# New piece costs in a kernel's planner, and a TensorE order searched with them

## The chip, the cores and the metric

The kernel runs on one core of one Trainium2 chip. A core has TensorE (matrix multiplies, here called PE), VectorE (DVE), ScalarE (ACT), GpSimd (POOL), a queue of transfers issued from SyncE (SP), and 16 DMA engines between HBM and the core's own memory. TensorE writes to eight banks of PSUM, from which VectorE and ScalarE copy. The metric is the device time of one execution in microseconds (us); lower is better.

## The reference: what is computed

Two layers of the same kind, each an attention with a recurrent memory followed by a gated feed-forward part, on 2048 tokens of width 576. All inputs are bfloat16. The same weights serve both layers.

```python
def _A_ref(x, mem0, Wq, Wk, Wv, Wo, seg_len):      # seg_len 32, M = 8, 32 heads of 128
    ...
    mem = mem0
    for s in range(n_seg):
        xs = x[:, s * seg_len:(s + 1) * seg_len, :].copy()
        h = jnp.concatenate([mem, xs], axis=1)
        q = jnp.einsum('btd,dhe->bhte', h, Wq)
        k = jnp.einsum('btd,dhe->bhte', h, Wk)
        v = jnp.einsum('btd,dhe->bhte', h, Wv)
        scores = jnp.einsum('bhqe,bhke->bhqk', q, k) * scale
        scores = jnp.where(mask[None, None], scores, -1000000000.0)
        p = _softmax(scores, axis=-1)
        o = jnp.einsum('bhqk,bhke->bhqe', p, v)
        o = jnp.einsum('bhte,hed->btd', o, Wo)
        mem = o[:, :M, :].copy()
        outs.append(o[:, M:, :])
    return jnp.concatenate(outs, axis=1)
...
x = x + _A_ref(_layernorm(x, axis=-1), A_mem0, A_Wq, A_Wk, A_Wv, A_Wo, A_seg_len)
x = x + _B_ref(_layernorm(x, axis=-1), B_w1, B_w3, B_w2)      # (silu(x w1) * (x w3)) w2, 576 -> 4608 -> 576
x = x + _A_ref(_layernorm(x, axis=-1), A_mem0, A_Wq, A_Wk, A_Wv, A_Wo, A_seg_len)
x = x + _B_ref(_layernorm(x, axis=-1), B_w1, B_w3, B_w2)
```

A segment needs the memory that the segment before it leaves, so the 64 segments of a layer come one after the other.

## The kernel before

**Steps.** The second layer runs 8 segments behind the first (`LAG`), so there are 72 steps, and in most of them one step works on a segment of each layer at once: 80 columns (two times 32 tokens and 8 memory columns) go through the same weights. At both ends, steps have one layer only and 40 columns. Heads are worked in four groups of eight. After every four steps the feed-forward part takes a group of 128 tokens of each layer; its weights don't fit beside the attention's and are loaded anew each time in pairs of 128-row blocks (`W13`, `W2C`).

**Pieces.** `make_nodes` (from line 236) lists all work as nodes: each has an engine (or "either ScalarE or VectorE"), an estimated duration, the nodes that it depends on, and the buffers that it takes and frees. On TensorE a node is a piece of 4 to 64 matmuls, and each kind has a letter: Q and q are QK's main part and tail (the width of 576 is four blocks of 128 rows and a tail of 64), S the scores, T a transpose of the softmax on TensorE, P the product with V, O and o the output projection and its tail, V, v, X, x, G, g the V projections, F and f the feed-forward's upper part, W and w its lower part for the first and second layer's tokens, and a, b, n, p the transposes around the layer norms. In steps with both layers the softmax is transposed by DMA instead of T (node `TRD`, from PB to PTS); its planned duration is `TRD` on the queue and `TRL` until it has landed.

**Modes.** A matmul can use the whole 128x128 array ("full"), or two halves of its columns ("col") or of its rows ("row"); the V pieces of the ends also use narrower forms ("c32", "oct", "quad"). Some kinds need one mode: Q and O full, q, f and g row, o and the scores of two layers col. Flexible ones are "full/col": F, W, w, G, P, T and the layer norms' transposes. In col mode the emitter splits each of their matmuls in two, one for each half of the columns.

**The planner.** `plan` (from line 80) goes through the nodes as a list scheduler: it keeps a clock for each engine, takes the node that can start first, and issues every engine's work in the order in which the nodes are planned. So its estimated times set the order on ScalarE, VectorE, GpSimd and SP, and which of ScalarE and VectorE does a copy. TensorE's own order is not chosen there: it is the string `ORDER`, FIRST, then FOUR eleven times, then LAST, one letter for each piece. `plan` adds `SWITCH` (98 ns) when the next piece has no mode in common with the run before it, narrows the run's mode to what all of its pieces share, and sets the mode when the run ends (`settle`). `MORE` holds additions by engine and kind, `LATS` the time from an engine's end to the start of a reader elsewhere. None of these numbers reaches the chip: they act through the order of the instructions, the choice between ScalarE and VectorE, the buffers' numbers and the mode of a piece.

The emitter's `mm` (line 622) records each matmul and splits it in col mode. All matmuls have line 627 in the profile, all ScalarE work line 630 and all VectorE work line 633; tiles tell them apart (HT,W is QK; QKT scores; PTS,V the product with V; OT,WO the output projection; XTB,W and W2C,HTT the feed-forward; WV,HT V).

Of the kernel before, what the change touches and what calls it, by code (L numbers as in the profile page):

```python
# [55 lines left out]
class Node:  # L56
    __slots__ = ("eng", "dur", "fn", "deps", "prio", "mode", "acq", "rel", "name", "lat", "outs", "left", "ready",
                 "start", "end", "by")

    def __init__(self, eng, dur, fn, deps=(), prio=0.0, mode=None, acq=(), rel=(), name="", lat=None):  # L60
# [19 lines left out]
def plan(nodes, pools, letters):  # L80
# [15 lines left out]
    both = []  # L96
    mode, run = [], []
    order = []
# [24 lines left out]
    while len(order) < len(nodes):  # L123
# [76 lines left out]
def ewh(*ns):  # L200
# [4 lines left out]
FIRST = (  # L205
    "maqqQqQSqTQQQSqQqqSQTQqSXxVvPPTTOOPoPOooOoQqqqqQQSQVvSqqQQQTQSqqXTSPOPTPOOTooPoxOoQQqqqqQSQvVqSQqQQQSqqTPSTOPoOT"
    "PTOPooOoaQqqQQSQqqVvSqQQQqqqTSQPxTSOPXOToToPPOOooQqqqpQQSVvqqQQnQSFfqqQTQSPfqFSOTFPfWoTOPFTOPoofOoFfqqQQWSFQQqqf"
    "vVqQSTFqfQWQQSqfqFPFTSXfPWTOPOxoTFoPOOffooFVqqvQQWQSQqqfFQqqfFSQTWSPQqfqFQFSTOfPWoTOPFTOPfaOoooFfqqQQvqqSQQWSfVF"
    "qQqQWQTQPqSqTOPbSOxxXTXTPooPOOooQpQQqqqqQSnQSFfqFfQvqVSfFWQqqQfPSFPOOooFfPWOFPofOoFQqqfqQWQSqqqQQQSFSGfgqQQqgfFP"
    "GSWPGfggfFFGOPoOOPWOoooFFffqqQQWSqqQQFvSqfVqQQfFSWqQQqfPPSFFOOPWoOffFPoaoOoWQqqqqQQbSQQQqqSGSgqQQqgPGSOPGggGoPOO"  # L210
    "PooOoQqqqppQQQqvVSSnnQFfqqQQQfqqSFFSPfPwOOWoFPoffFOwPWOooFqqffQQwFWQQqqFSSFffqqQQQQqqwWSSgfGFPGgggGPGOoPOOPWOooo"
    "wFqfqqQQQQSffqqFFSQQwvqVWSFQqqffFQWPwSFffPOPOOowooWFPFOoafQQqqqWSQqqqQQQSwSbQqQgqGSggGPGPOGoPgOPOOooo"
)
# [4 lines left out]
LAST = (  # L218
    "QqqppQQSQqqqvVSQQnqqnQSFPqffQOoSPFOFPwWOFPfooOofQQQqqqfFSwWQQFfqqfFSwWqqQQSGqffgFQFPGgWSwPFggfGOOPoGowPOOooFvfqq"
    "VQQQQSWqqFSFqqffQQQQqqSPwWSFfPOOoWwFffPFPOOooowQWQfqqqFSFfqqQQQWSqqqQQSQbvVVSPwXvxPOPOoOPooOoQQppVqqqQQSqvqnQSnQ"  # L220
    "qffFFQTSqqQTPwFfSPWTOOPFffTFooOPWwOooFffqvVQWFQQqqqQSwSQQfqqFSTFfqqQQWTPwSPFOTOffoPTFoPOOWoowxvXVqqQQFSQqfqqQQSF"
    "QQqqqfQTwPSTSWOPFOffTFPToWoPOwOooFqqfvQQQSQqqfVwWSFFfQqqQTWqSPQQqTOSPbOxooTXPTwPOOooQQpqqqQSqQVvnSqqQQqQSQFfqTFP"
    "STfOPoTOwPTFPOOooofVvqqQQQqqSQQSFfqqFQQSTwqqQTFPffSPOTOwxXooPTFPOOffooFQQqqqqQSQFSfvVqqQQQTqqSQwTPfSOFPFTOwTooPf"
    "POfOooFvVQQqwQqqqSQqqQSQfFTSqQqQfPTSPOOooFTTPPfOOoopwfFFnFwffFFwffFFwwffFfFwFfFwffFfFwFfFwffFFwffFFwffFw"
)
# [10 lines left out]
def make_nodes(em, nseg, pools, o=Opt, dma_bw=230e3, load_bw=400e3):  # L236
# [125 lines left out]
    def step(t):  # L362
# [18 lines left out]
        for g in range(NG):  # L381
            qs, qe = [], []
            for u in (2 * g, 2 * g + 1):
                q = Slot("qkt", users=1)
                b = banks()
                pq = t + o.qk + o.ustep * u
                m_ = node("PE", 32 * mm80, em.qk(t, u, b), deps=hx + hm[:1] + ([ld_h[u // 4]] if t == 0 else []),
                          prio=pq, mode="full", acq=[q] + b, name="QK")
                n = node("PE", 4 * mm80, em.qk_tail(t, u, b), deps=hx + hm + ([ld_h[u // 4]] if t == 0 else []), prio=pq + o.qkt, mode="row",
                         acq=[q] + b, name="QKt")  # L390
# [22 lines left out]
            if nl == 2 and g < DMA_GROUPS:  # L413
                pe_ = [node("DMA", TRD, em.ptd(t, g, pb, pts), deps=[pbs], prio=pf, acq=[pts], rel=[pb], name="TRD", lat=TRL)]
                pts_of[t, g] = pe_[0]
            else:
                bt = banks(nl)
                tr = node("PE", 8 * (0.0258 if nl == 1 else 0.0358), em.ptr(t, g, pb, bt), deps=[pbs], prio=pf + o.tr, mode="full/col", acq=[pts] + bt, rel=[pb], name="TR", lat=0.265)
# [14 lines left out]
            wo = node("PE", 32 * mm80, em.wo(t, g, ot), deps=ote + ([ld_o[g]] if t == 0 else []), prio=t + o.wo + o.wog * g, mode="full",  # L433
                      acq=[y] if g == 0 else [], name="WO")
# [35 lines left out]
    def job(j):  # L470
# [36 lines left out]
        for at, pp in enumerate([npp - 1] + list(range(npp - 1)) if last else range(split, npp)):  # L507
# [5 lines left out]
            for pr_ in (2 * pp, 2 * pp + 1):  # L513
# [18 lines left out]
                fm = node("PE", 16 * mm, em.ffn_up(ents, pr_, w13, b, last and not stays, False), deps=wr + ld, prio=prio, mode="full/col",  # L532
                          acq=b + [htt], rel=rel13, name="FF")
                ff = node("PE", 2 * mm, em.ffn_up(ents, pr_, w13, b, last and not stays, True), deps=wr + ld, prio=prio + o.fft, mode="row",
# [6 lines left out]
            for (bi, g) in ents:  # L541
                b = banks()
                d = node("PE", 8 * 0.1225, em.ffn_down(em.col(bi, g), pp, htts, w2s, b, last and not stays), deps=mids + lds, prio=prio + o.w2,
                         mode="full/col", acq=b, rel=htts + w2s, name="W2b" if bi else "W2")
                if last and at == npp - 1:
# [847 lines left out]
```

## Time and profile before

| | |
|---|---|
| median of 3 runs | 2644.31 us |
| lowest, highest run | 2639.14, 2650.45 us |
| profiled execution, its own time | 2638.71 us |
| its span (first to last instruction) | 2636.9 us |
| mean granted TensorE clock | 0.996 |
| read from HBM, over the span | 306.72 MB, 117 GB/s |

The profile is of one execution. Busy time of an engine is the time in which at least one of its instructions ran; matmuls overlap in the array, and their ends are modelled, so the start of one piece to the start of the next tells more of its cost than its listed length. The chain of waits follows the last instruction back to what released it, step by step. A wait is listed with the engine and line that waited, what it waited for, and the total, the number and the longest. Numbers such as 128*64 in a matmul's shape are the rows and columns of the array that it used, so 128*64 is col mode, 64*128 row mode and 128*128 full.

### The profile page before, as it was taken

The numbers are of one execution on the slowest core, as the hardware profiler recorded it, in microseconds if no ns is written. First come the engines' busy times: TensorE is split into PE (matmuls) and PEld (weight loads), VectorE is DVE, ScalarE is ACT, GpSimd is POOL, SyncE is SP. The second block draws the span as 40 slices with busy tenths as digits, with TensorE's granted clock in tenths as the row PEclk, the third lists the DMA queues.
The fourth block names the chain that finished last, engine by engine and source line by source line (L and its number), as shares of the span: only waits on it lengthen the run. The fifth ranks groups of instructions, "written<-read, shape, count | busy, mean of one in ns | idle before, by whom it ended". The sixth has DMA issues, their size and how long they took to land.

```text
span 2636.9 us, 134690 instructions
## 1 busy us (share of the span) xinstructions
PE 2574.1 (98%) x60031; PEld 2222.3 (84%) x60031; DVE 2004.5 (76%) x5137; ACT 1264.2 (48%) x3745; POOL 196.7 (7%) x253
## 2 busy tenths in 40 slices
PE   5999999999999999999999999999999999999998
PEld 4788888889888888888888888888888888888886
DVE  4787777887778678777877777787777777777876
ACT  2655553444445454444545444454545445454552
POOL 1100000000000010000001001000100001010000
PEclk9999999999999999999999999999999999999999
DMA  9065755575464656546454654655465464545357
GB/s 324 4 174 135 190 104 147 130 148 139 126 147 115 139 127 155 136 131 151 113 140 116 159 140 128 155 110 139 114 156 143 132 159 94 139 122 146 106 156 247
DMA packets 683207, 371.56 MB, mean 141 GB/s; under 512 B 233753, under 2 KB 672801, under 8 KB 681985
## 3 DMA queue, kind: packets, MB, share of 16 engines
q1 hardware_dynamic: 678944, 355.00, 53.2%
q8 instruction: 469, 7.68, 1.2%
q0 software_dynamic: 3024, 6.93, 0.9%
q10 hardware_dynamic: 656, 1.02, 0.2%
q14 instruction: 114, 0.93, 0.1%
HBM read 306.72 MB, written 2.36 MB: 117 GB/s over the span
## 4 chain that ended last, share of the span: by engine, by line
PE 91%; DVE 4%; DMA 3%; issue 1%; ACT 1%; ACTq 0%; DVEq 0%; SPq 0%
PE bank L627 91%; DMA PTS<-PB 2%; DVE HTT L633 1%; DVE PB L633 1%; DVE STAT L633 1%; DMA WV<-in_A_Wv_dram 0%; DVE SME L633 0%; DMA W<-in_A_Wk_dram 0%; DVE V L633 0%; DVE QKT L633 0%; DMA W2C<-in_B_w_dram 0%; DVE XR L633 0%; ACT HTT L630 0%; ACT HT L630 0%; DVE LNS L633 0%
## 5 line engine op out<-in xcount | busy, mean ns | idle before, releaser
L627 PEld LDWEIGHTS <-W 128*128 128x128 bf16 (+2 forms) x32920 | 1261.8, 101 | 119.8 <-issue 67.8
L627 PE MATMUL bank<-HT,W 128*128 128x80 bf16 (+3 forms) x23040 | 795.2, 197 | 21.3 <-ACT HT L630 8.2
L627 PE MATMUL bank<-XTB,W 128*64 128x256 bf16 (+5 forms) x9880 | 658.4, 264 | 2.1 <-issue 1.3
L630 ACT ACTIVATE QKT<-bank 128x256 bf16<-128x256 f32 (+4 forms) x1676 | 385.1, 309 | 302.9 <-PE bank L627 296.5
L627 PE MATMUL bank<-OT,WO 128*128 128x80 bf16 (+3 forms) x11520 | 411.6, 198 | 2.5 <-issue 1.9
L627 PEld LDWEIGHTS <-WO 128*128 128x128 bf16 (+1 forms) x11520 | 383.2, 102 | 29.9 <-issue 16.3
L630 ACT ACTIVATE V<-bank 64x512 bf16<-64x512 f32 (+1 forms) x603 | 338.0, 584 | 137.4 <-PE bank L627 131.4
L627 PE MATMUL bank<-WV,HT 128*32 128x512 bf16 (+4 forms) x3576 | 363.5, 384 | 0.3 <-issue 0.2
L627 PE MATMUL bank<-W2C,HTT 128*64 128x288 bf16 (+1 forms) x3440 | 323.8, 287 | 0.5 <-DMA W2C<-in_B_w_dram 0.5
L630 ACT ACTIVATE HTT<-bank 128x512 bf16<-128x512 f32 (+1 forms) x322 | 172.6, 551 | 300.1 <-PE bank L627 299.1
L633 DVE TENSOR_REDUCE STAT<-SME 104x8 f32<-104x320 f32 (+1 forms) x576 | 274.9, 477 | 28.2 <-ACT SME L630 21.2
L633 DVE TENSOR_TENSOR PB<-SME,STAT 40x128 bf16<-40x128 f32 (+4 forms) x912 | 274.8, 335 | 9.3 <-DMA PTS<-PB 0.5
L627 PEld LDWEIGHTS <-HT 128*32 128x32 bf16 (+4 forms) x3576 | 149.2, 99 | 147.7 <-issue 37.8
L633 DVE SCALAR_TENSOR_TENSOR HTT<-HTT,bank 128x512 bf16<-128x512 bf16 (+1 forms) x322 | 201.0, 624 | 94.4 <-ACT HTT L630 91.6
L627 PEld LDWEIGHTS <-HTT 128*64 128x64 bf16 (+1 forms) x3512 | 233.1, 106 | 31.2 <-DVE HTT L633 4.1
L1047 POOL MEMSET PB<- 128x1024 bf16 x142 | 135.0, 952 | 1657.0 <-DMA PTS<-PB 1114.3
L633 DVE SCALAR_TENSOR_TENSOR XR<-bank,XR 128x288 f32<-128x288 f32 x574 | 240.0, 447 | 20.3 <-PE bank L627 17.2
L630 ACT ACTIVATE OT<-bank 128x320 bf16<-128x320 f32 (+1 forms) x383 | 144.4, 404 | 214.5 <-PE bank L627 185.3
L630 ACT ACTIVATE SME<-SME 104x320 f32<-104x320 f32 (+1 forms) x288 | 135.5, 470 | 194.3 <-DVE SME L633 192.4
L633 DVE TENSOR_TENSOR HTT<-HTT,bank 128x512 bf16<-128x512 bf16 (+1 forms) x322 | 203.3, 631 | 28.5 <-PE bank L627 1.4
L633 DVE CAST V<-bank 64x512 bf16<-64x512 f32 (+1 forms) x261 | 178.9, 686 | 40.1 <-PE bank L627 34.9
L633 DVE TENSOR_TENSOR SME<-bank,maskb 104x320 f32<-104x320 f32 (+1 forms) x288 | 138.5, 482 | 53.8 <-PE bank L627 50.1
(59 smaller groups left out, 1383.5 us busy)
## 6 DMA issues: line engine op xcount, KB each, us to landing
W<-in_B_w_dram SPq DMA_DIRECT2D x608, 256.0 KB, 3.6
W2C<-in_B_w_dram SPq DMA_DIRECT2D x304, 288.0 KB, 3.4
W<-in_B_w_dram SPq DMA_DIRECT2D x608, 32.0 KB, 3.4
W<-in_B_w_dram SPq DMA_DIRECT2D x8, 1024.0 KB, 12.6
W<-in_A_Wq_dram SPq DMA_DIRECT2D x9, 512.0 KB, 9.9
WO<-in_A_Wo_dram SPq DMA_DIRECT2D x4, 1152.0 KB, 19.1
XR<-in_A_x_dram POOLq DMA_DIRECT2D x16, 288.0 KB, 3.1
WV<-in_B_w_dram SPq DMA_DIRECT2D x4, 1152.0 KB, 7.5
```

The source lines that it names most:

```text
L627: self.ch("PE", self.nc.tensor.matmul(out, lhsT=lhsT, rhs=rhs, start=start, stop=stop, skip_group_check=True, **k))
L630: self.ch("ACT", self.nc.scalar.activation(*a, **k))
L633: self.ch("DVE", getattr(self.nc.vector, fn_)(*a, **k))
L1047: return lambda n: self.ch("POOL", self.nc.gpsimd.memset(self.pbt(pb), 0.0))
```

## The change

It touches numbers of the planner, one rule in it, and the order string. No computation, buffer or transfer is added or removed.

- Node gets a field `wide`: an extra cost of a flexible piece if its run ends up col. `plan` adds these up over a run and charges them once the run can only be col.
- `wide` is set for VG (0.01 us), TR (0.04), PV (0.014 with two layers, 0.045 with one), FF (0.02) and W2 (0.01).
- Costs of single pieces change: scores of two layers, WO tails and VG count less; scores of one layer, QK and WO of one layer and QK tails count 8 to 22 ns more.
- Transfers are planned shorter: the transposed softmax's landing 2.1 us after its 1.3 on the queue instead of 2.3, W13 and W2 loads 0.2 us shorter.
- FIRST, FOUR and LAST have the same letters as before, each in another order.

```diff
-        "PE": {"SC": 0.05, "WOt": 0.03, "VG": 0.03, "FFt": 0.01, "TR": 0.01, "QK": 0.007}}
+        "PE": {"SC": 0.0, "WOt": 0.022, "VG": 0.003, "FFt": 0.01, "TR": 0.01, "QK": 0.007}}
...
-TRD, TRL = 1.3, 2.3
+TRD, TRL = 1.3, 2.1
...
-        self.lat = lat
+        self.lat, self.wide = lat, wide
...
-    mode, run = [], []
+    mode, run, owed = [], [], 0.0
...
                 dur += SWITCH
                 settle()
-                mode = n.mode
+                mode, owed = n.mode, 0.0
             mode = [m for m in mode if m in n.mode]
+            owed += n.wide
+            if mode == ["col"]:
+                dur += owed
+                owed = 0.0
             run.append(n)
...
 FOUR = (
-    "QqqqppQvVSQQnnQFqfqFSfqqQQFfqQSWPwPSFffOOowFPWoOPFOooFqfqfQQwQQqqgSWGSFqqfQQQPwQSWFqffqFSGgggGPGPOOwooOPWOooFFqq"
-    "ffQQQQSwVvqqfFSQQqqWPFSFfqqfQQwOSWPFFoffPOOWPwOoooFfqqQQqqaSQQqWSQQqqqQQSbwSggGGPGPOggoGPOPOOooo"
+    "QqqqppQVvSQQnnQqqFSffqFQQQqqfSFPWwSPOFoffOFPwWOPFOoooFqffqQQQQqqSWwGSFfqqgQQQPWQSwFffqqFGSgggGPGOPoOwFPOWOoooFqq"
+    "ffQQQWSVfqqvQFQQqqSwPFSFffqqQQWOSwPoFFffPOOwPWOoooFfqqQQqqaSQQWqqSQqqQQQSbwSggGGPGPOoggGPOPOOooo"
 )
...
-        m_ = node("PE", 8 * 0.2158, em.vg(t, g, b, False), deps=deps, prio=t + o.vm, mode="full/col", acq=b, name="VG")
+        m_ = node("PE", 8 * 0.2158, em.vg(t, g, b, False), deps=deps, prio=t + o.vm, mode="full/col", acq=b, name="VG", wide=0.01)
...
-                m_ = node("PE", 32 * mm80, em.qk(t, u, b), deps=hx + hm[:1] + ([ld_h[u // 4]] if t == 0 else []),
+                m_ = node("PE", 32 * mm80 + (0.02 if nl == 1 else 0.0), em.qk(t, u, b), deps=hx + hm[:1] + ([ld_h[u // 4]] if t == 0 else []),
...
-            sc = node("PE", 8 * (0.0312 if nl == 2 else 0.029), em.scores(t, g, qs, s), deps=qe, prio=pf + o.sc, mode="col" if nl == 2 else "full/col", acq=[s, sme], rel=qs, name="SC")
+            sc = node("PE", 8 * (0.0305 if nl == 2 else 0.038), em.scores(t, g, qs, s), deps=qe, prio=pf + o.sc, mode="col" if nl == 2 else "full/col", acq=[s, sme], rel=qs, name="SC")
...
-                      prio=pf + o.pv, mode="full/col", acq=b + [ot], rel=[pts], name="PV")
+                      prio=pf + o.pv, mode="full/col", acq=b + [ot], rel=[pts], name="PV", wide=0.014 if nl == 2 else 0.045)
...
-                    ld = [node("DMA", kb(1152, 256) / dma_bw, em.load_w13(pr_, w13), prio=prio - 1, acq=[w13], lat=2.5, name="W13")]
-                    lds.append(node("DMA", kb(256, 576) / dma_bw, em.load_w2(pr_, w2), prio=prio - 0.99, acq=[w2], lat=2.4, name="W2l"))
+                    ld = [node("DMA", kb(1152, 256) / dma_bw, em.load_w13(pr_, w13), prio=prio - 1, acq=[w13], lat=2.3, name="W13")]
+                    lds.append(node("DMA", kb(256, 576) / dma_bw, em.load_w2(pr_, w2), prio=prio - 0.99, acq=[w2], lat=2.2, name="W2l"))
```

More of the change, by code (lines that the diff above doesn't have):

```diff
@@ L57, with __init__ @@
     __slots__ = ("eng", "dur", "fn", "deps", "prio", "mode", "acq", "rel", "name", "lat", "outs", "left", "ready",
-                 "start", "end", "by")
-    def __init__(self, eng, dur, fn, deps=(), prio=0.0, mode=None, acq=(), rel=(), name="", lat=None):
+                 "start", "end", "by", "wide")
+    def __init__(self, eng, dur, fn, deps=(), prio=0.0, mode=None, acq=(), rel=(), name="", lat=None, wide=0.0):
         self.eng, self.dur, self.fn, self.prio, self.mode = eng, dur, fn, prio, mode.split("/") if mode else mode
@@ L211 @@
[L211 to L212 removed]
+    "maqQqQQqSQqQqqSQqqQTQSTSXvxVPPOTOToPoPOOooQqqqqQQSQQSqvqVQqTSQqTPQOSPXoTOPTOPoxoOoQQqqqqQSQvVqqSQQqqQQSSTTPPOoOT"
+    "aTPoPOOooQQvqqVqqSQQQSQqqQQTSqqxPTSOPXOTTPooPOOooQqqpQQSQVqqqvnSQFfqQFTSQqfqPTQFSPOfoTOPWOTFPooffOoFQQqqqqQWSQFS"
+    "FffqvVQQqqqQWQTSTSPFFffXWTPOoxTPOFPOOoooffFQWQqqqqQSQFSQqffvVFqWQQqfSTFTQfqFPSaPOWTofFOPTFPOOoooWQqqfQQSQqqVSvFf"
@@ L213 @@
+    "qQTWQQqqqTPSQObSPoXXTTxxPOPOOoooQpQqqqqQQnSSvfqfFVFqQQQSFfqqWQfSPPFOOoFfPWOofoPFOoFfqqQQWQQqfqSFSQQqgqqGSQQPFqgf"
+    "GWSfFPOFofggGGPOWPOOFoooffFQQqqqWSqQQFqvSfVQQqqWSQfqFQfPSFPOOooaPWFffOPFOooWQqqqqQQbSQQQqqSGSqgqQQPgGSOoPGggGPOO"
+    "PooOoQQppQqqqqQVSnSnqvQFfqfQFQQfqqSFSWPwPOFOooffFPwOPWOooFfqqQQFSqfqQQwQWQSFqqffFGwWSfgqFPQQqGSgggGPGPOOOWoaoPow"
+    "OFoFfqfqQQQwQSWFqqffFSvVqqQQFwPSfqqQWQFSffPOOPFwWooOPFOoofQQqqqWSQqqqQQSQwbqqSQQGggSgGPGPOogGPOPOOooo"
 )
 FOUR = (
-    "QqqqppQvVSQQnnQFqfqFSfqqQQFfqQSWPwPSFffOOowFPWoOPFOooFqfqfQQwQQqqgSWGSFqqfQQQPwQSWFqffqFSGgggGPGPOOwooOPWOooFFqq"
@@ L221 @@
[L221 to L224, printed above, removed]
+    "QqqqppQQQqSVvnSnqqQQQFSfqqQPFOSofPFOPwWOFPfooOofQQWQqqqwSFffqqFQQQwWFfgqGSSfQPFQFqqfgGwWPOSofggFGGPOFPOOoooWfqQQ"
@@ new lines @@
+    "wQQvqqqVSSFfqqQQFwqqfQQWSSfPFPOFOwWoffPFPOOoooWwqqQQFSqffFQQqqWSQqqqQQQvSSVVbPwPOXvOPooxPOOooQvqqppQVqQSQqqQnnQS"
+    "FfqqQQqfSFTSTFwPWOPToffFTPOPOOooowQWFQqqfVqqvQSQFSQfqfqFQWwSTQQFffqqFTPSwWOFPFTTOPooffPOOooXxvqqVQQwWSQQQqqqqQSF"
+    "QqqffFSTTQPWwSFPOTFPToffOPOOwoooWVqqfvQQFSQqfqQWwFSFfqqTQQWqqSTPQQOPSboOTXPxoTOPwOooQQqqpQSQvqqVSQnqqqQQSqfTQfTP"
+    "SFPOTOFPooTOPwOooFFvqffVQQqqqQSQwSQFqqfQTQFPSTfqqQOPSxFwTXoPTOPOOoooFffqQQqqqQSQQSFQvfqqVwqSQqQFTTSFfPPTOofPwTOP"
+    "OOfoooFVvQqqQwSQqqqqQQSFfqqQQSQTTSFPPOOfooTTfPPOOoopwfFFnFwffFFwffFfFwwfFfFwFffFwFfFwffFfFwFfFwffFFwffFw"
@@ L386, in step @@
                 pq = t + o.qk + o.ustep * u
-                m_ = node("PE", 32 * mm80, em.qk(t, u, b), deps=hx + hm[:1] + ([ld_h[u // 4]] if t == 0 else []),
+                m_ = node("PE", 32 * mm80 + (0.02 if nl == 1 else 0.0), em.qk(t, u, b), deps=hx + hm[:1] + ([ld_h[u // 4]] if t == 0 else []),
                           prio=pq, mode="full", acq=[q] + b, name="QK")
-                n = node("PE", 4 * mm80, em.qk_tail(t, u, b), deps=hx + hm + ([ld_h[u // 4]] if t == 0 else []), prio=pq + o.qkt, mode="row",
+                n = node("PE", 4 * mm80 + (0.014 if nl == 1 else 0.008), em.qk_tail(t, u, b), deps=hx + hm + ([ld_h[u // 4]] if t == 0 else []), prio=pq + o.qkt, mode="row",
                          acq=[q] + b, name="QKt")
@@ L417, in step @@
                 bt = banks(nl)
-                tr = node("PE", 8 * (0.0258 if nl == 1 else 0.0358), em.ptr(t, g, pb, bt), deps=[pbs], prio=pf + o.tr, mode="full/col", acq=[pts] + bt, rel=[pb], name="TR", lat=0.265)
+                tr = node("PE", 8 * (0.0258 if nl == 1 else 0.0358), em.ptr(t, g, pb, bt), deps=[pbs], prio=pf + o.tr, mode="full/col", acq=[pts] + bt, rel=[pb], name="TR", lat=0.265, wide=0.04)
                 pe_ = [node("AD", ew(320), em.pt_ev(t, g, i, b, pts), deps=[tr], prio=pf, rel=[b], name="PTe") for i, b in enumerate(bt)]
@@ L432, in step @@
             ote = [node("AD", ew(4 * c80), em.ot_ev(t, g, ab, b[ab], ot), deps=[pv], prio=pf, rel=[b[ab]], name="OTe") for ab in (0, 1)]
-            wo = node("PE", 32 * mm80, em.wo(t, g, ot), deps=ote + ([ld_o[g]] if t == 0 else []), prio=t + o.wo + o.wog * g, mode="full",
+            wo = node("PE", 32 * mm80 + (0.016 if nl == 1 else 0.0), em.wo(t, g, ot), deps=ote + ([ld_o[g]] if t == 0 else []), prio=t + o.wo + o.wog * g, mode="full",
                       acq=[y] if g == 0 else [], name="WO")
@@ L543, in job @@
                 d = node("PE", 8 * 0.1225, em.ffn_down(em.col(bi, g), pp, htts, w2s, b, last and not stays), deps=mids + lds, prio=prio + o.w2,
-                         mode="full/col", acq=b, rel=htts + w2s, name="W2b" if bi else "W2")
+                         mode="full/col", acq=b, rel=htts + w2s, name="W2b" if bi else "W2", wide=0.01)
                 if last and at == npp - 1:
```

9 lines of the change are left out of this document (1 added, 8 removed).

## The prediction

> **What bounds the kernel now.** I read the page first: engine shares, then the chain of work that ended last.
>
> ```profile
> span 2636.9 us, 134690 instructions
> PE 2574.1 (98%) x60031; PEld 2222.3 (84%) x60031; DVE 2004.5 (76%) x5137; ACT 1264.2 (48%) x3745; POOL 196.7 (7%) x253
> PE 91%; DVE 4%; DMA 3%; issue 1%; ACT 1%; ACTq 0%; DVEq 0%; SPq 0%
> ```
>
> TensorE is busy 98% of the span and is 91% of the chain that sets the end; VectorE and ScalarE have a quarter and a half of their time free. So an edit counts by what it does to TensorE: the work it issues, and the little time it waits. To see where it waits I cut the span at the ends of the order's parts: start-up, rest of FIRST, two of the eleven repeated blocks (FOUR), LAST. Columns: length, then busy time of TensorE matmuls, weight loads, VectorE, ScalarE, GpSimd, then granted clock, DMA share, GB/s.
>
> ```profile
> 0.00:60.00 60.00, 30.72 (x727) 23.27 (x729) 28.07 (x68) 15.15 (x39) 8.20 (x20) 0.94 1.00 350
> 60.00:522.50 462.50, 450.40 (x11687) 384.49 (x11684) 358.48 (x958) 238.17 (x709) 36.92 (x45) 0.99 0.51 127
> 675.98:828.45 152.47, 152.13 (x3409) 132.63 (x3409) 116.95 (x298) 73.83 (x222) 11.15 (x14) 1.00 0.53 136
> 981.13:1134.04 152.91, 152.30 (x3408) 132.56 (x3408) 117.05 (x298) 73.88 (x222) 11.20 (x14) 1.00 0.57 135
> 2203.32:2631.76 428.44, 417.14 (x10132) 354.87 (x10131) 329.00 (x831) 198.80 (x567) 28.48 (x34) 1.00 0.55 150
> ```
>
> Length less busy time: TensorE idles 29.3 us in the first 60 (the DMA engines are full there, share 1.00), 12.1 in the rest of FIRST, 0.3 to 0.6 in a block (5 over eleven) and 11.3 in LAST. Outside start-up that is some 28 us, about 1% of the span. The list of waits says for what, in the eleven blocks together (us in total, times, longest):
>
> ```profile
> PE bank L627 <- ACT HT L630: 3.8, 11, 0.3
> PE bank L627 <- DMA PTS<-PB: 1.6, 6, 0.3
> ```
>
> One wait of 0.3 us per block, for the memory columns that carry one segment to the next, and now and then a transposed P that has not landed (0.27 us each, 1.6 / 6). So the blocks are TensorE work, not waiting.
>
> **The change part by part.** The pieces of work stay the same: the old and new strings hold the same letters (773, 208 and 664). What changes is the order, and through it how often the array is re-tiled and which flexible pieces run column-tiled. I applied the planner's own rule to both strings (a run of pieces keeps a mode as long as they share one; a piece that could be either takes the run's). Mode switches go from 1270 to 1223: 302 to 293 in FIRST, 66 to 64 in each block, 242 to 226 in LAST. By the mode that is left: column-tiled 323 to 311, full 433 to 409, row-tiled 408 to 397, the V pieces' narrower forms 105 both times (the first piece of all enters a mode without leaving one). Flexible pieces that run column-tiled fall by 162: FFN up 215 to 154, V 42 to 30, PV 103 to 61, P transposes on TensorE 15 to 9, FFN down 151 to 110. Each issues half as many matmuls when full, so 60,031 matmuls become 58,247.
>
> Prices come from the timeline of TensorE in one block. A matmul's listed length overlaps the next one's, so I take start to start of neighbouring pieces; columns are start, length, shape, count.
>
> ```profile
> 1011.48 1.91 PE L627 MATMUL bank<-XTB,W 128*64 128x256 bf16 x32
> 1013.23 0.45 PE L627 MATMUL bank<-PTS,V 128*64 128x80 bf16 x16
> 1013.51 1.15 PE L627 MATMUL bank<-W2C,HTT 128*64 128x288 bf16 x16
> 1014.50 1.56 PE L627 MATMUL bank<-OT,WO 128*64 128x80 bf16 x40
> ...
> 1016.60 1.91 PE L627 MATMUL bank<-XTB,W 128*128 128x256 bf16 x16
> 1018.35 1.72 PE L627 MATMUL bank<-OT,WO 128*128 128x80 bf16 x48
> ...
> 1041.71 1.96 PE L627 MATMUL bank<-XTB,W 128*64 128x256 bf16 x32
> 1043.61 0.32 PE L627 MATMUL bank<-HT,W 64*128 64x80 bf16 x8
> 1043.76 0.60 PE L627 MATMUL bank<-XTB,W 64*128 64x256 bf16 x8
> 1044.20 0.31 PE L627 MATMUL bank<-HT,W 64*128 64x80 bf16 x8
> ...
> 1055.36 1.15 PE L627 MATMUL bank<-W2C,HTT 128*128 128x288 bf16 x8
> 1056.44 1.73 PE L627 MATMUL bank<-OT,WO 128*64 128x80 bf16 x48
> 1058.00 0.45 PE L627 MATMUL bank<-PTS,V 128*128 128x80 bf16 x8
> 1058.29 1.15 PE L627 MATMUL bank<-W2C,HTT 128*128 128x288 bf16 x8
> 1059.27 1.72 PE L627 MATMUL bank<-OT,WO 128*128 128x80 bf16 x48
> 1060.82 3.66 PE L627 MATMUL bank<-XTB,W 128*64 128x256 bf16 x64
> 1064.41 0.46 PE L627 MATMUL bank<-HT,W 64*128 64x80 bf16 x16
> 1064.71 0.60 PE L627 MATMUL bank<-XTB,W 64*128 64x256 bf16 x8
> 1065.24 1.93 PE L627 MATMUL bank<-HT,W 128*128 128x80 bf16 x49
> ```
>
> **A switch.** FFN down in full mode takes 0.98 (1058.29 to 1059.27) before another full piece and 1.08 (1055.36 to 1056.44) before a column-tiled one: leaving full costs 0.10. Two row-tiled FFN tails take 0.44 (1043.76 to 1044.20) before row-tiled work and 0.53 (1064.71 to 1065.24) before full work: leaving row costs 0.09. A column-tiled FFN up takes 1.75 (1011.48 to 1013.23) within its run; at the end of a run it takes 1.90 (1041.71 to 1043.61), and in a pair 3.59 - 1.75 = 1.84 (1060.82 to 1064.41): leaving column mode costs 0.09 to 0.15, and I take the middle. Gain: 12 x 0.12 + 24 x 0.10 + 11 x 0.09 = **4.8 us**, with bounds 4.5 and 5.2. It all lies on TensorE, which is the chain, so nothing hides it except where TensorE waits anyway (a rival below).
>
> **Column-tiled against full.** FFN up: 1.75 tiled, 1.75 full (1016.60 to 1018.35). PV: 0.28 tiled (1013.23 to 1013.51), 0.29 full (1058.00 to 1058.29). FFN down: 0.99 tiled, 0.98 full. Twice the matmuls run in pairs, side by side, in the same time, so the 1,784 matmuls that vanish are worth nothing by themselves: 162 x 0.00, with bounds of 162 x 0.01 = 1.6 us either way. V and the P transposes have no row here; the nearest, FFN up and PV, stand for them.
>
> The weight loads show where a difference could sit:
>
> ```profile
> L627 PEld LDWEIGHTS <-V 128*128 128x128 bf16 x1480 | 66.4, 99 | 27.4 <-issue 9.5 <-ACT V L630 2.4 <-DMA PTS<-PB 1.6
> ...
> L627 PEld LDWEIGHTS <-V 128*64 128x64 bf16 x1648 | 45.3, 112 | 6.8 <-issue 2.6 <-DMA PTS<-PB 1.3
> ```
>
> A load of half the columns takes longer (112 ns against 99), and there are twice as many. The Trainium skill (TensorEngine Tiling (Array Packing), Restrictions and Gotchas) says that column tiling excludes the fast weight load. If a PV piece were bound by its loads, a tiled one would cost 16 x 112 to 8 x 99, 2.3 times a full one, an estimate from that page's rule and these two rows, and 42 PV pieces turned full would be worth 42 x 0.28 x 1.3 / 2.3 = 6.6 us more: 11.4 gained instead of 4.8. The starts above contradict it (0.28 and 0.29), so it gets no chance of its own.
>
> **What moves.** Reordering moves the evictions on ScalarE and VectorE, the transposes and weight loads on SP's queue, and the x loads and stores on GpSimd's, all of which the planner issues in the order in which it thinks they start. Which waits are exposed depends on how much TensorE work stands between a producer and its reader. I laid the durations above along both strings. In a block the least work between a group's scores and its PV is 8.8 us before and 9.1 after; between a PV and the output projection that reads it, 1.0 both times (one FFN down piece). Both blocks end in the three output tails followed at once by the next segment's QK, so the 0.3 us wait at the seam stays. In FIRST and LAST some distances grow and others shrink by a few tenths. I take 1 us less waiting; bounds: half of the 28 us saved, or the case of late landings below.
>
> **The shorter transfer times in the planner.** These change no transfer, only when the planner believes in it. The transposes' landing times (us, lowest, median, highest):
>
> ```profile
> DMA to landing us min/median/max: 2.6/3.3/6.0
> ```
>
> The planner counted 1.3 + 2.3 = 3.6 and now counts 3.4, still above the median. If one is late, the PV that reads it waits, and since TensorE issues in order, everything behind it: 0.27 us each time by the row above. The weight loads are shortened by the same 0.2. Where a PV is put right behind its planned landing this costs; the block's least distance says it is not put closer.
>
> **Sum.** The profiled execution took 2638.71 us, 1.8 around its span of 2636.9: 2638.71 - 4.8 - 1 = 2632.9. That execution is at the low edge of the runs shown (2639.14 to 2650.45, median 2644.31); carried to the median, 2644.31 - 5.8 = **2638.5**.
>
> **The rivals.** (1) *The waits go too.* The reordering has 28 us of idle time to work on outside start-up; if half goes, 14 + 4.8 = 19 us and 2625. For it: FIRST and LAST each idle 11 to 12 us and are rewritten the most. Against: the distances between producer and reader there move both ways.
> (2) *The switches vanish where TensorE waits anyway.* 25 of the 47 are in FIRST and LAST, where TensorE idles 2.6% of the time; if none of those counts, only the blocks' 22 x 0.10 = 2.2 us is left: 2642. Against: the idle time there sits in a few dozen spots, not at every switch.
> (3) *Slower: PV waits for late transposes.* The planner trusts every landing 0.2 us more, and with a highest of 6.0 some land far beyond 3.4. If half of the 224 transposes (16 a block, the rest at both ends) were each waited for at 0.27, that is +30 - 4.8 = +25: 2670. It decides from 18 such waits on (4.8 / 0.27), where the gain is used up, and from 67 the kernel is slower by more than 0.5%. For it: the blocks repeat, so one bad spot is paid eleven times. Against: six waits of 176 today, and more distance at the tightest spot.
> (4) *The change does not do what it says*: the new numbers are no nearer to the chip. That ends at no change, like (2), since the switches fall whatever the numbers are.
>
> **How the numbers follow.** The forecast has a chance of 0.55, and its own range is 2633 to 2645 (waits 6 us either way). Rival 1 has 0.17, rivals 2 and 4 together 0.16, rival 3 has 0.12. 0.5% of the median is 13 us, about what a measurement tells from no change. Faster by more than that needs 8 us of waits beside the switches: most of rival 1 and an edge of the forecast, 0.19. Slower needs 67 late waits: most of rival 3, 0.10. Within: 0.71. The range runs from 2627 (the switches and 12.5 us of the waits saved) to 2651 (rival 3 with 43 late waits, less the gain); the far ends of rivals 1 and 3, some 2 in 10, are left out.
>
> **What would show it.** The switches: a block of some 152.4 us where 152.5 to 152.9 stood, with 3,312 matmuls. The column-tiled pieces: 58,247 matmuls in all; these counts fall to 4,512, 896 and 1,760 with the starts per piece unchanged:
>
> ```profile
> L627 PE MATMUL bank<-XTB,W 128*64 128x256 bf16 x6240 | 373.9, 273 | 0.0
> L627 PE MATMUL bank<-W2C,HTT 128*64 128x288 bf16 x2416 | 177.7, 287 | 0.5 <-DMA W2C<-in_B_w_dram 0.5
> ...
> L627 PE MATMUL bank<-PTS,V 128*64 128x80 bf16 x1376 | 41.0, 202 | 1.5 <-DMA PTS<-PB 1.5
> ```
>
> The waits: idle time near 12 us in the rest of FIRST and 11 in LAST, and waits for PTS near six in the blocks. I am wrong if a full piece takes less time than its tiled form, if a switch saved is not time saved, or if waits for PTS, HT or HTT grow by more than 5 us.

## The result, and the profile after

| | before | changed |
|---|---|---|
| median of 21 runs, side by side | 2641.06 us | 2637.77 us |
| lowest and highest | 2636.38, 2650.45 | 2633.89, 2643.18 |
| ratio to before, with its 95% interval | | 0.998 (0.9974 to 0.9987) |
| span of the profiled execution | 2636.9 us | 2632.6 us |

The changed kernel is faster by 0.2%: 5.3 us by the ratio, 3.4 to 6.9 by its interval, while the two medians lie 3.3 us apart. That is clear of noise, and well under 0.5%.

The page and the same stretches of the changed kernel, cut again where FIRST, the eleven blocks and LAST begin (columns as before: length, then busy time of TensorE matmuls, weight loads, VectorE, ScalarE, GpSimd, granted clock, DMA share, GB/s):

```profile
span 2632.6 us, 131011 instructions
PE 2570.7 (98%) x58247; PEld 2209.5 (84%) x58247; DVE 2026.5 (77%) x5189; ACT 1249.3 (47%) x3693; POOL 196.3 (7%) x253
```

```profile
0.00:60.00 60.00, 31.70 (x698) 22.65 (x698) 27.41 (x66) 14.88 (x37) 8.26 (x20) 0.89 0.99 350
60.00:521.64 461.64, 449.55 (x11407) 382.86 (x11407) 358.14 (x969) 236.33 (x702) 36.89 (x45) 1.00 0.51 127
521.64:2199.94 1678.30, 1672.03 (x36432) 1452.35 (x36432) 1309.77 (x3311) 801.69 (x2399) 123.12 (x154) 1.00 0.56 135
2199.94:2627.45 427.51, 416.13 (x9706) 350.98 (x9705) 329.56 (x840) 196.40 (x558) 28.02 (x34) 0.99 0.55 150
```

And the eleven blocks before, in one row:

```profile
522.49:2203.32 1680.83, 1674.54 (x37489) 1459.09 (x37489) 1287.30 (x3278) 812.13 (x2432) 123.15 (x154) 1.00 0.56 135
```

Take busy from length. TensorE's idle time in the rest of FIRST was 12.1 us and is 12.1; in the blocks it was 6.3 and is 6.3; in LAST 11.3 and 11.4. What fell is the busy time: 450.40 to 449.55, 1674.54 to 1672.03 and 417.14 to 416.13, together 4.4 us, and the span is 4.3 us shorter. In the first 60 us, where the granted clock is 0.89 instead of 0.94, busy time is 1.0 us longer and idle time 1.0 shorter. So in this pair of profiles and behind the start-up, the gain is work that TensorE no longer has, not waiting. One pair can't settle a microsecond of waiting, though. A second profile of the changed kernel, taken on another chip (e15 below), idles 9.6 us in the rest of FIRST:

```profile
60.00:518.67 458.67, 449.10 (x11419) 382.79 (x11414) 358.44 (x969) 236.94 (x703) 36.93 (x45) 1.00 0.51 127
```

VectorE has 22 us more work in the blocks and ScalarE 10 us less: the planner gave some copies to the other engine, and TensorE waits no more for it.

The waits of the matmuls in the blocks (total, times, longest; in the changed kernel line 631 has the matmuls, 634 ScalarE's work and 637 VectorE's):

```profile
PE bank L631 <- ACT HT L634: 3.8, 11, 0.3
PE bank L631 <- DMA PTS<-PB: 1.4, 3, 0.7
PE bank L631 <- DMA W<-in_B_w_dram: 0.7, 3, 0.3
```

The seam's 0.3 us stands in each block as before. Waits for transposes went from six to three (in the whole run from eleven, 5.0 us, to seven, 4.7), and three short ones for feed-forward weights are new.

```profile
L631 PE MATMUL bank<-XTB,W 128*64 128x256 bf16 x4512 | 273.0, 273 | 0.3 <-DMA W<-in_B_w_dram 0.3
L631 PE MATMUL bank<-W2C,HTT 128*64 128x288 bf16 x1760 | 127.1, 288 | 0.0
...
L631 PE MATMUL bank<-PTS,V 128*64 128x80 bf16 x896 | 28.0, 202 | 0.0
```

The counts of column-tiled matmuls are those worked out from the strings.

### The profile page after: what moved, and what is told of

The parts are those of the page before. It is cut to its first block, busy times and chain, and to the rows that moved or that the text cites. A ratio compares the mean times of both kernels' runs of the same rounds, so it can differ in the third digit from the quotient of the medians.

```text
span 2632.6 us, 131011 instructions
## 1 busy us (share of the span) xinstructions
PE 2570.7 (98%) x58247; PEld 2209.5 (84%) x58247; DVE 2026.5 (77%) x5189; ACT 1249.3 (47%) x3693; POOL 196.3 (7%) x253
## 4 chain that ended last, share of the span: by engine, by line
PE 92%; DMA 4%; DVE 3%; issue 1%; ACT 1%; SPq 0%; ACTq 0%; DVEq 0%
PE bank L631 92%; DMA PTS<-PB 1%; DMA W<-in_B_w_dram 1%; DMA W<-in_A_Wk_dram 1%; DVE HTT L637 1%; DVE STAT L637 1%; DVE SME L637 0%; DVE PB L637 0%; DMA XN<-in_A_x_dram 0%; SPq L640 0%; DVE V L637 0%; DMA W2C<-in_B_w_dram 0%; ACT HT L634 0%; DVE QKT L637 0%; ACT HTT L634 0%
## 5 line engine op out<-in xcount | busy, mean ns | idle before, releaser
L634 ACT ACTIVATE QKT<-bank 128x256 bf16<-128x256 f32 (+2 forms) x1648 | 376.1, 311 | 289.5 <-PE bank L631 264.0
L634 ACT ACTIVATE V<-bank 32x512 bf16<-32x512 f32 (+1 forms) x585 | 331.4, 585 | 123.5 <-PE bank L631 116.1
L631 PE MATMUL bank<-W2C,HTT 128*64 128x288 bf16 (+1 forms) x3112 | 317.5, 287 | 0.4 <-DVE HTT L637 0.3
L637 DVE CAST V<-bank 64x512 bf16<-64x512 f32 (+1 forms) x279 | 191.5, 686 | 41.5 <-PE bank L631 35.1
L637 DVE CAST QKT<-bank 128x192 bf16<-128x192 f32 (+4 forms) x400 | 109.5, 317 | 84.8 <-PE bank L631 82.3
```

Source lines behind the costliest of these rows:

```text
L631: self.ch("PE", self.nc.tensor.matmul(out, lhsT=lhsT, rhs=rhs, start=start, stop=stop, skip_group_check=True, **k))
L634: self.ch("ACT", self.nc.scalar.activation(*a, **k))
L637: self.ch("DVE", getattr(self.nc.vector, fn_)(*a, **k))
```

## The experiments

All ratios are to the kernel before, on the same chip in the same job; chips differ (before took 2631.63 us beside the first four, 2639.52 and 2639.22 beside the others), so times are compared within a job only. Profiles of different chips are set side by side below, and there a difference of a few microseconds outside the blocks says little.

### Strings and numbers apart

The change has two halves, so each was run without the other.

```diff
  e1: the changed kernel with FIRST, FOUR and LAST of before
  e2: the kernel before with FIRST, FOUR and LAST of the changed one
```

> The new planner numbers with the old order strings. Theory A (the gain is the 47 mode switches that the new strings save on TensorE, 4.3 us): no gain here; TensorE issues what it issued before, so a block of the repeated part takes 152.7 to 152.9 us as before and the whole is within 2 us of before, up to 3 us more if copies come a little later. Rival B (the numbers themselves help, because they are nearer to the chip): 2 to 5 us less than before. Rival C (string and numbers belong together: the planner orders VectorE's and ScalarE's copies by where it believes each piece of TensorE stands, and with a string made for other numbers a copy comes behind the wrong neighbour in every block): more than 1% slower than before, with one TensorE wait of 1 us or more that comes back in each of the eleven blocks.

> The old planner numbers with the new order strings. Theory A (the strings alone carry the gain): as the changed kernel within 2 us, 4 to 5 us less than before; blocks of 152.1 to 153.2 us. Rival B (the numbers carry it): as before within 2 us. Rival C (string and numbers belong together): more than 1% slower than before, with a TensorE wait of 1 us or more that comes back in each block, for transposed PTS or for a copy of VectorE or ScalarE.

Measured: e1 2680.27 us, ratio **1.0181** (1.0168 to 1.0195); e2 2680.79 us, ratio **1.0185** (1.0164 to 1.0207). Each half alone costs nine times what both together gain. Theory A and rival B fall, and rival C's loss and its waits in each block are there. The blocks of e1 and then of e2, one row each:

```profile
522.01:2229.20 1707.19, 1679.66 (x37489) 1460.12 (x37488) 1309.89 (x3355) 794.12 (x2355) 123.35 (x154) 1.00 0.53 133
```

```profile
530.59:2230.77 1700.18, 1675.66 (x36432) 1451.93 (x36432) 1310.69 (x3311) 801.25 (x2399) 122.91 (x154) 1.00 0.54 134
```

Idle time of TensorE rises from 6.3 us to 27.5 and 24.5, though it issues the same matmuls in the same order as the kernel whose string it has. What it waits for in the blocks, in e1 and then in e2:

```profile
PE bank L631 <- DVE XN L637: 12.5, 12, 1.1
PE bank L631 <- DVE OT L637: 7.5, 11, 0.7
```

```profile
PE bank L627 <- DMA PTS<-PB: 18.4, 17, 2.2
```

One wait for XN and one for OT in each block of e1, and transposes in e2. Profile against profile, the blocks hold only part of the loss: e1's are 26.4 us longer than before and its LAST 16.7, e2's are 21.9 us longer than the changed kernel's, its FIRST 9.0 and its LAST 8.4. The two ends were not followed wait by wait. In the blocks, the timeline of each run shows an instruction out of place. In e1, VectorE's order around the norm whose output TensorE transposes (start, length, operation):

```profile
1276.91 0.15 DVE L637 TENSOR_SCALAR LNS<-LNS 128x1 f32<-128x1 f32 x1
...
1277.88 0.56 DVE L637 CAST QKT<-bank 128x192 bf16<-128x192 f32 x2 [0.19 <-PE bank L631]
1278.36 1.05 DVE L637 TENSOR_TENSOR PB<-SME,STAT 40x320 bf16<-40x320 f32 x3
1279.44 0.49 DVE L637 TENSOR_TENSOR SME<-bank,maskb 104x320 f32<-104x320 f32 x1
1279.85 0.57 DVE L637 TENSOR_SCALAR XN<-XR,LNS 128x576 bf16<-128x576 f32 x1
```

and the same place before (a reduction and a reciprocal are left out in both):

```profile
1267.66 0.15 DVE L633 TENSOR_SCALAR LNS<-LNS 128x1 f32<-128x1 f32 x1
...
1268.47 0.58 DVE L633 TENSOR_SCALAR XN<-XR,LNS 128x576 bf16<-128x576 f32 x1
```

With its own string the norm starts 0.81 us after the last of its inputs on VectorE (1267.66 to 1268.47), with the wrong numbers 2.94 us after it (1276.91 to 1279.85): two copies, three products and a mask addition were planned in between, and VectorE does them first while TensorE waits. In e2 it is SP's queue (start, length until the last was issued):

```profile
1246.74 6.93 SPq L636 DMA_DIRECT2D W<-in_B_w_dram  x8
1253.78 1.26 SPq L1050 DMA_TRANSPOSE PTS<-PB  x1
```

and the same two pieces in the changed kernel:

```profile
1234.95 1.26 SPq L1054 DMA_TRANSPOSE PTS<-PB  x1
1236.30 5.12 SPq L640 DMA_DIRECT2D W<-in_B_w_dram  x8
```

and, in e2, the last six of those eight transfers and VectorE's products that fill that PB:

```profile
1249.49 4.19 SPq L636 DMA_DIRECT2D W<-in_B_w_dram  x6
```

```profile
1249.34 1.12 DVE L633 TENSOR_TENSOR PB<-SME,STAT 40x128 bf16<-40x128 f32 x4
```

In e2 two W13 loads (eight transfers) stand ahead of the transpose and hold the queue for 6.9 us. Only 1.7 us of that, between the second transfer (issued by 1247.77) and the third (1249.49), is a wait for TensorE to give back a W13 buffer. The rest is the issuing itself, 0.5 to 1.3 us for each transfer; the last six take 4.19 us in a row. VectorE had written that PB by 1250.46 (1249.34 + 1.12), when the queue had four of them still to issue, so the transpose goes out 3.3 us late, and the PV behind it waits.

### The two places mended by hand

```diff
  e8, on e2: after the plan is made
+    for n in [n for n in seq if n.name == "TRD" and 20 <= n.prio < 64 and int(n.prio) % 4 == 2 and 0.05 < n.prio % 1 < 0.08]:
...
+        for m in loads:            # the W13 loads right ahead of it on SP's queue
+            seq.remove(m)
+        j = seq.index(n) + 1
+        seq[j:j] = loads
  e9, on e1: after the plan is made
+    for p in [n for n in seq if n.name == "L1pow"]:
+        n, = p.outs
+        seq.remove(n)
+        seq.insert(seq.index(p) + 1, n)
```

> Old numbers with the new order strings, as in e2, but in ten of the eleven blocks the two W13 loads that stand on SP's queue right ahead of the third step's second transpose are put right behind it, after the plan is made; everything else stays. Theory F (that transpose is ready and stands behind loads that wait for TensorE to give back a W13 buffer, so the PV waits for PTS): the repeated wait of 0.7 to 2.4 us at that PV goes, 10 x 1.6 = 16 us less than e2, with blocks of 152.5 to 153.5 us. Rival G (VectorE writes PB too late): less than 4 us less than e2.

> New numbers with the old order strings, as in e1, but VectorE's layer norm of the second layer's input is put right behind GpSimd's power that it needs, after the plan is made, ahead of the copies and products that the planner had put between; everything else stays. Theory H (VectorE's order makes the transposes of that norm wait on TensorE, 1.32 us in each block, and the V piece behind them 0.85): 11 x 1.32 = 14.5 us less than e1, or 24 with the second wait; blocks of 152.5 to 153.6 us. Rival I (the chain itself is late, because its input comes late from TensorE): less than 3 us less than e1.

Measured: e8 2702.12 us, ratio 1.0233 (1.0215 to 1.025); e9 2695.39 us, ratio 1.0212 (1.0198 to 1.0227). Both are slower than what they mend, and neither theory had that. Yet each edit did what it should at its place. In e8 the start of that PV after the piece before it comes 0.7 to 2.5 us sooner in ten blocks, 15.6 us together, as forecast. In e9 the step from the scores to the norm's transposes is 1.32 us shorter in all eleven, 14.6 us together. The time came back behind it: in e8 the next PV starts 0.4 to 3.4 us later after its neighbour in nine blocks, and the FFN up pieces wait for the loads that were put back; in e9 the V piece a little later, whose wait should have gone too, starts 1.25 us later after the PV before it in each block, 13.9 us together. The waits in the blocks, e8 first, then e9:

```profile
PE bank L627 <- DMA PTS<-PB: 22.9, 15, 3.3
PE bank L627 <- DMA W<-in_B_w_dram: 7.4, 9, 1.9
```

```profile
PE bank L631 <- DVE OT L637: 10.5, 11, 1.0
PE bank L631 <- DVE V L637: 9.0, 11, 0.8
```

Part of what came back is the clock. In e9, TensorE idles twice in each block just ahead of that V piece, 0.8 and 0.95 us, and in six of the eleven blocks the V piece then runs at a granted clock of 0.5 and takes 0.9 to 1.6 us longer. The V piece of the fifth block, that of the sixth, and the stretch of the fifth with its clock (the third figure from the end):

```profile
1299.54 3.54 PE L631 MATMUL bank<-WV,HT 128*128 128x512 bf16 x8 [0.95 <-DVE OT L637]
```

```profile
1456.23 1.89 PE L631 MATMUL bank<-WV,HT 128*128 128x512 bf16 x8 [0.95 <-DVE OT L637]
```

```profile
1299.60:1303.00 3.40, 3.40 (x10) 1.23 (x10) 2.48 (x6) 0.42 (x1) 0.95 (x1) 0.50 0.30 68
```

e8's blocks have six such stretches of 3.4 us, those of e1 and e2 none. With the same matmuls, TensorE's busy time in the blocks is 6.8 us longer in e8 than in e2 (1682.45 against 1675.66), and 8.1 us longer in e9 than in e1 (1687.80 against 1679.66).

So the misplaced instruction is real, and it is not alone: other copies and transfers are out of step with the string too, and what is put forward pushes back what stood there.

### Which numbers

```diff
  e6, on the changed kernel: three piece costs of before
-        "PE": {"SC": 0.0, "WOt": 0.022, "VG": 0.003, "FFt": 0.01, "TR": 0.01, "QK": 0.007}}
+        "PE": {"SC": 0.05, "WOt": 0.03, "VG": 0.03, "FFt": 0.01, "TR": 0.01, "QK": 0.007}}
...
-            sc = node("PE", 8 * (0.0305 if nl == 2 else 0.038), ...
+            sc = node("PE", 8 * (0.0312 if nl == 2 else 0.029), ...
  e7, on e2: the same two lines the other way round
  e10, on the changed kernel
-TRD, TRL = 1.3, 2.1
+TRD, TRL = 1.3, 2.3
...
-                dur += owed
+                dur += 0.0
...
  (W13 lat 2.3 -> 2.5, W2l lat 2.2 -> 2.4)
  e13, on the changed kernel: QK, QKt and WO without their extras, as before
```

> The changed kernel (new order strings, new wide costs, new transfer times, new extras of one-layer pieces) with the old costs of three pieces alone: scores, V pieces in full width, and the output projection's tails. Theory C1 (string and numbers belong together, and it is these three costs: the planner's TensorE runs 1.2 us later by the end of a block): 1.5% to 2.7% slower than before, with a wait for PTS that comes back in each block, as with all old numbers. Rival C2 (the transfer times or the wide costs are what the new string needs): within 0.5% of the changed kernel.

> The old numbers but for those three costs, which are the new ones, with the new order strings: no wide costs, transposes landing 2.3 us after the queue, weight loads 0.2 us later, no extras of one-layer pieces. Theory C1: as the changed kernel within 3 us, so 2 to 8 us less than before. Rival C2: 1% slower than before or more. If theory C1 holds, trusting each landing 0.2 us more is worth nothing either way.

Measured: e6 2682.43 us, ratio 1.0165 (1.0151 to 1.0179); e7 2640.91 us, ratio 1.0004 (0.9996 to 1.0012). Three costs, the scores', V's and the output tails', spoil the changed kernel when they alone go back, and PV waits for PTS at the same place in every block again. Given alone to the old numbers they mend the blocks but not the whole: by the ratios e7 lies some 6 us above the changed kernel, though its blocks last 1677.80 us against 1678.30. Its span is 7.2 us longer (2639.8), 4.0 us of it in FIRST and 3.7 in LAST; that is one profile of each, on two chips, and the changed kernel's own two profiles differ by 3 us in FIRST (521.64 and 518.67). So theory C1 holds for the blocks only.

> The changed kernel with the old transfer times (transposes landing 2.3 us after the queue, weight loads 0.2 us later) and no wide costs; the three new piece costs and the extras of one-layer pieces stay. The kernel with the three piece costs alone kept the blocks at 152.07 us but lost 4.1 us in FIRST and 3.7 in LAST. Theory J (what it lacked there are the extras of one-layer pieces, which only FIRST and LAST hold): as the changed kernel within 2 us, 3 to 7 us less than before. Rival K (the transfer times and wide costs matter at the ends): 5 us or more above the changed kernel, so no gain over before.

> The changed kernel without the extras of one-layer pieces (20 ns of QK, 14 of its tail, 16 of WO, and 8 of the two-layer QK tail); all else new. Theory J: 4 to 8 us above the changed kernel, all of it in FIRST and LAST, with blocks as before this edit. Rival K: as the changed kernel within 2 us.

> The changed kernel once more, beside the other two, for how much of a block's length changes from one execution to the next. Theory A: 0.1% to 0.3% less than before. If the waits above the seam's 0.4 us in a block (0.5 us in the mean, for PTS and weights) come from landing times that scatter, they fall on other blocks this time and the shortest block stays at 152.1 us; if they come from the order, they fall on the same places.

Measured: e10 2638.31 us, ratio 0.9997 (0.9988 to 1.0005); e13 2639.62 us, ratio 0.9999 (0.9991 to 1.0008); the changed kernel beside them 2634.18 us, ratio 0.9979 (0.9971 to 0.9988). Theories J and K are both right, or nearly, in what they claim for their own numbers (by the ratios e13 lies 5.3 us above the changed kernel and e10 4.8, where K asked for 5) and wrong in what they deny the other's: either set alone, taken back, loses the whole gain. Profile against profile, with the changed kernel of the same job, e10 is 3.8 us longer in FIRST, 2.5 in the blocks and 2.2 in LAST; e13 is 6.5 longer in FIRST, not in the blocks (1678.67 us against 1678.87), and 3.0 in LAST. With one profile of each, the split is rough. Which of e10's three numbers does it was not tried apart. The second profile of the changed kernel has the same shortest block, 152.06 us, and its waits fall partly on the same places (before the scores in the first, sixth and eleventh block both times) and partly on others, so landing times that scatter are at most a part of it.

### The price of a switch

```diff
  e3, on the changed kernel
     for n in plan(nodes, pools, ORDER):
+        if n.name == "FF" and n.mode == "col":
+            n.mode = "full"
         em.mode = n.mode
```

> The changed kernel with every FFN up piece that ran column-tiled (154 of them) emitted full, after the plan is made, so that the order on every engine stays the same. The switches rise from 1222 to 1386 (16, 143 and 5 more in the three strings). Theory A (a switch costs about 0.10 us on TensorE and is not hidden; a tiled piece costs as much as a full one): 164 x 0.105 = 17 us more than the changed kernel, 12 us more than before, a block 1.3 to 1.4 us longer. Rival D (switches fall into waits): less than 8 us more. Rival E (a tiled piece is dear by itself, 0.02 to 0.04 us, as the planner's new numbers count it): 17 - 154 x 0.03 = 12 us more than the changed kernel, a block 1.0 us longer.

Measured: 2642.09 us, ratio 1.0039 (1.0027 to 1.0052), so 0.59% or some 15.6 us above the changed kernel by the quotient of the two ratios; 17 were expected. The ends of the two intervals leave 11 to 21 us, which rules out rival D but not rival E's 12. The order of every engine is the changed kernel's, so here the planner plays no part. A block of e3, and its eleven blocks together:

```profile
1136.57:1290.00 153.43, 153.09 (x3120) 129.78 (x3120) 119.08 (x301) 72.93 (x219) 11.21 (x14) 1.00 0.55 134
...
521.54:2210.82 1689.28, 1684.73 (x34320) 1427.71 (x34320) 1309.86 (x3311) 802.16 (x2399) 123.20 (x154) 1.00 0.53 134
```

The shortest block is 153.43 us and six of the eleven are within 0.01 us of it; the changed kernel's shortest is 152.06:

```profile
1133.39:1285.45 152.06, 151.72 (x3313) 132.00 (x3312) 119.05 (x301) 72.89 (x219) 11.20 (x14) 1.00 0.57 136
1285.45:1438.69 153.24, 152.41 (x3312) 132.19 (x3312) 119.12 (x301) 72.90 (x219) 11.20 (x14) 1.00 0.58 135
```

13 more switches, 1.37 us: 0.105 each, with 192 matmuls fewer. That is theory A. The mean of the blocks, 153.57 (1689.28 / 11) against 152.57 (1678.30 / 11), is 1.0 us longer, which would be rival E. But these profiles are from two chips, and the changed kernel's blocks vary by 1.2 us, as its two rows show, because scattered waits add to most of them. A fairer mean comes from the next run, e4, on e3's chip: its blocks hold the changed kernel's instructions, since its edit reaches no piece of a block.

```profile
517.92:2193.22 1675.30, 1670.42 (x36432) 1452.10 (x36432) 1309.94 (x3311) 801.94 (x2399) 123.21 (x154) 1.00 0.55 136
```

1689.28 less 1675.30, over 143 switches, is 0.098 each and 1.27 us a block, nearer to theory A.

```diff
  e4, on the changed kernel, where a run of pieces could be either mode
-            x.mode = mode[0]
+            x.mode = "col" if "col" in mode else mode[0]
```

> The changed kernel with the 21 runs that could be either mode (38 of their pieces FFN up and down, nearly all in the last 45 us) column-tiled instead of full; switches and every engine's order stay. Theory A (a tiled piece costs nothing within a run, leaving column mode for row mode costs 0.137 and leaving full mode 0.095): 21 x 0.04 = 0.9 us more in the last 45 us, all of it at the ends of the runs. Rival E (0.02 to 0.04 us for each tiled piece): 0.8 to 1.5 us more, spread over the starts within the runs.

Measured once: 2634.65 us. That is 3.0 us above the median of before beside it (2631.63, with runs from 2628.69 to 2634.49), where the changed kernel takes 3.4 to 6.9 us less than before. So by this one run it is some 6 to 10 us slower than the changed kernel, and neither theory had that. Piece by piece, both theories have a part. At the runs' ends an FFN up piece of 128 tokens mostly takes 17 ns more before row mode when tiled (1017 against 1000), and an FFN down piece 1 to 53 ns more (1128 against 1076 in one); the mean of these fourteen is 20, half of theory A's 40. Within a run FFN up mostly takes 14 ns more (917 against 903) and FFN down the same (980). Over the 34 pieces that can be compared it is 0.5 us.

The rest is idle time. LAST and what follows it, in e4 and then in the changed kernel:

```profile
2193.22:2632.90 439.68, 418.18 (x10175) 354.48 (x10174) 331.65 (x843) 196.17 (x558) 28.14 (x34) 1.00 0.51 146
```

```profile
2199.94:2632.60 432.66, 417.46 (x9714) 351.60 (x9713) 331.22 (x843) 196.40 (x558) 28.02 (x34) 0.99 0.54 149
```

It is 7.0 us longer (6.6 against the changed kernel's second profile, 433.06), and 6.3 of that is idle time of TensorE (439.68 - 418.18 against 432.66 - 417.46). From 2500 us on, TensorE's gaps that the profile puts to nothing ("issue") are, in the same order:

```profile
PE bank L631 <- issue: 13.6, 13, 2.9
```

```profile
PE bank L631 <- issue: 5.9, 5, 2.4
```

Some of these gaps lie inside a tiled FFN up piece. The second profile of the changed kernel has 6.0 us in five gaps there. So tiled pieces may cost more in this place than their starts tell; with a single run and no cause in the profile, that stays open.

## Why the prediction was right

The time forecast, 2638.5 us, lies 0.7 us from the median measured, 2637.77, and a change within 0.5% had the largest chance. That the two times lie so close is luck: the forecast started from 2644.31, a median of three runs, and before took 2641.06 in the larger set. The fair comparison is the difference: 5.8 us forecast, 4.3 in the spans, 5.3 (3.4 to 6.9) by the ratio.

**The switches.** 4.8 us forecast (4.5 to 5.2); TensorE's busy time fell by 4.4, or 0.093 us a switch. By stretch: 2.5 for the blocks' 22, 0.9 for FIRST's nine (after the first 60 us) and 1.0 for LAST's sixteen, where 1.6 were due. The shortest block went from 152.30 us, the row below, to 152.06, or 0.12 for each of its two switches:

```profile
1134.04:1286.34 152.30, 151.96 (x3408) 132.62 (x3408) 116.82 (x298) 73.84 (x222) 11.20 (x14) 1.00 0.52 136
```

e3 shows the price by itself, 0.098 to 0.105. Rival 2, that the switches of FIRST and LAST would vanish in waits, is not what the rows show for FIRST: idle time there did not rise, and busy time fell. In LAST, up to its last instruction, busy time fell from 418.46 to 417.46 in one profile and to 418.02 in the other, so some of its sixteen may have vanished so.

**Tiled against full.** Forecast at nothing, within 1.6 us either way. e4 puts it at 0 to 14 ns for most pieces within a run, and e3's blocks lost 192 matmuls each without a gain beyond the switches' price. What e4 lost in gaps at the end is not explained; over the whole run these gaps ("issue") were 9.2 us before and 9.7 after, so the change did not gain by them. 42 PV pieces turned full as said, and TensorE's busy time fell by about the price of the switches. The estimate of 6.6 us more, which goes by the rule in the Trainium skill (TensorEngine Tiling (Array Packing), Restrictions and Gotchas) that column tiling excludes the fast weight load, is not seen in it.

**The waits.** 1 us less was forecast. Behind the start-up TensorE idled 33.5 us before and 33.6 in the first profile of the changed kernel, but 31.1 in the second, so the term is neither shown nor refuted: it is smaller than what two executions of one kernel differ by. Rival 1 asked for half of 28 us. That sum took 5 us for the eleven blocks, which from two of them was too little: they idled 6.3.

**Landings trusted sooner.** Rival 3 needed 18 waits for late transposes to undo the gain; the blocks have three. But the step that called the shorter transfer times worth nothing ("the block's least distance says it is not put closer") is right only for the pair of string and numbers as it came: with the old times and no wide costs (e10) the same string loses all it gained.

**Where the working fell short.** Rival 4 said that if the numbers were no nearer to the chip, "that ends at no change, like (2), since the switches fall whatever the numbers are". e2 is that case, and it is 1.85% slower. The prediction laid the two strings against each other as TensorE's work, and took the order of VectorE, ScalarE and SP's queue to follow along. It does not: here each string was good only with the numbers with which the planner, from that string, places some thousands of copies and transfers in a good order, and the prediction had no row that could tell that this pair was one. The forecast held because both halves came together, not because the numbers had been shown harmless. In that it was luck.

## What to carry to other kernels

Where one engine is busy 98% of the time, count what a change adds to or takes from that engine's own work, pieces and mode switches included, at prices read start to start; the idle time may hardly move. Where a planner orders several engines from estimated times, the estimates and the order of the main engine are one object: test them together, and don't carry half of it over, since here 1.2 us of estimate in a block of 152 made the kernel 1.65% slower than before. When a wait has a misplaced instruction behind it, moving that instruction can move the wait and not the time; look at what stood where it goes, and at the granted clock, which can make a wait cost more than its length. And set a run beside the kernel before of its own chip: e4's span is within 0.3 us of the changed kernel's from another chip, and hid a loss.

## What the runs showed of the hardware

- In e2 a transpose that was ready went out 3.3 us late, because the transfers ahead of it on the same queue were still being issued, six of them in 4.19 us; the queue did not pass them.
- Leaving column-tiled mode costs more than leaving the others. In the blocks, the scores of two layers take 0.24 to 0.27 us within a run and 0.34 to 0.39 at its end, and a tiled FFN up piece 1.73 to 1.77 and 1.85 to 1.90: some 0.12 us, against 0.09 to 0.10 from full or row. That is the prediction's middle.
- After TensorE had idled 0.82 and 0.95 us in short succession, the granted clock was 0.50 for 3.4 us in six of e9's eleven blocks, and a V piece took up to 3.54 us instead of 1.89. The same waits in the other five blocks left the clock at 1.00.
- In two profiles of the changed kernel, some dozen scattered waits of over 0.15 us beside the seams (12 and 14) made its blocks last 152.06 to 153.70 us. Only the shortest block repeats, 152.06 in both, and also in e4 and e13, which issue the same blocks on TensorE.
